# A new order of the instructions in the first fifteen slots of a fused attention and two-layer kernel

## The chip, the cores and the metric

The kernel runs on one core of a Trainium2 chip. The metric is the device time of one execution in microseconds. A core has five engines with queues of their own that work strictly in order: TensorE (PE in the profile; its weight loads are PEld), VectorE (DVE), ScalarE (ACT), GpSimd (POOL) and SyncE (SP), which here only issues DMAs. They meet through semaphores. TensorE writes to PSUM, eight banks of 128 x 512 floats, and another engine has to carry each result out before its bank can be written again.

## The reference

```python
def sm_attn(qq, kk, vv):                      # softmax attention, scale 1/8
    s = scale * qq @ kk.transpose(0, 1, 3, 2)
    a = np.exp(s - s.max(-1, keepdims=True))
    return (a / (a.sum(-1, keepdims=True) + 1e-9)) @ vv
pp  = sm_attn(p, k, v)                        # 8 batches x 8 heads, 32 packed rows x 64
out = sm_attn(q, pp, pp)                      # 576 rows per batch and head
x   = out.transpose(0, 2, 1, 3).reshape(4608, 512)
h = x @ w1_in;  y = (h * np.cos(h)) @ w1_out  # 512 -> 2048 -> 512
h = y @ w2_in;  g = P(h) / (Q(h) + 1e-6)      # P cubic; Q = 1 + |b0||h| + |b1|h^2
result = g @ w2_out                           # 4608 x 512
```

The four weight matrices arrive as 64-bit floats.

## The kernel before

**Stages.** First the packed attention (pp) of all batches, together with the second attention of batch 0 and the first conversions of weights, up to about 105 us. Then 128 *slots* for the first layer, eight batches of 576 rows, 16 slots a batch: a slot is one half of a batch's rows (288) and two blocks of 128 of the 2048 hidden columns. Last the second layer over 9 tiles of 512 rows. This case is about slots 0 to 14, between about 105 and 255 us of the span.

**Products in three passes.** Where the reference has one product of floats, the kernel has three with operands split into a rounded high part and the rest, hi x hi, hi x lo, lo x hi (`PASSES`). A split (`split`, `words_out`) is a copy on ScalarE (gh, hi of w1o, ah, yh) and a subtraction on VectorE or GpSimd (gl, lo of w1o, al, yl).

**W'.** The second attention's value product and the first layer's input product are merged: W' = pp x w1_in, per batch and head. It is made in 40 *units* (`wunit0` for batch 0, `wunit` for four or three other batches at a time). A unit of `wunit` is two matmuls into two PSUM banks of tag w, of which there are two in all. One half is scaled and copied out by ScalarE (line 316), the other by VectorE (line 314), into tiles `wev` (four), and a DMA writes them to the scratch `wd` (line 317). `fill(m)` issues m units.

**A slot** (`slot`, `chain1`, `mm_h`, `mm_y`). TensorE computes h (12 matmuls, line 614) into one tile of two banks, then y of the slot two back (24 matmuls in two halves, line 678) into the four banks y0 to y3, with units of W' between. The chain of the slot turns h into g = h cos h: ScalarE u (639), VectorE r (640), ScalarE absolute value and sine (645, 646), VectorE g (647). The split of g into gh and gl (66, 67, `finish_g`) is made in the chain of the *next* slot. From slot 11 (`LATE`) there are no units and h has two tiles.

**Conversions.** `conv_in` turns one block of 64-bit words (`words_in`) into floats: ScalarE (77), VectorE twice (79, 84), GpSimd (88). For w1_out the split by `words_out` (ScalarE 92, GpSimd 93) is put into a list, and `conv_out` issues one of it. The blocks come in the order of `steps`: f0 to f15 of w1_out, x8 to x15 of w1_in. y of slot n needs f blocks 2j and 2j+1. Slots 0 to 10 convert two blocks each (`conv_by`).

**Attention of batch 1** (`attn2_beside`) runs as a generator beside these slots: per head group a transpose of q (749, 753), scores on TensorE (763) with transposes back (771), maximum (777) and subtraction (778); then the exponential (783), sums (787 to 789), division (794), transposes (797) and splits (802, 812). `EARLY1` and `LATE1` say in which slots it is resumed.

**Order.** On TensorE, VectorE and ScalarE the instructions of this stretch stand in the order in which the code is written (`manual_schedule`); on GpSimd and SyncE a scheduler orders them.

Of the kernel before, what the change touches and what calls it, by code (L numbers as in the profile page):

```python
# [20 lines left out]
def pack_attention_moe_moe_kernel(  # L21
# [14 lines left out]
    nc = tc.nc  # L36
# [76 lines left out]
    if True:  # L113
# [152 lines left out]
        def ppt(n):  # L266
# [3 lines left out]
            for u in range(2):  # L270
# [7 lines left out]
                    out=to, in_=ps[r].rearrange("p (x u m) -> p u x m", u=2, m=M)[:, u], func=AF.Copy  # L278
                )

        def wunit0(fq, g):
            ps = psw.tile([128, 512], F32, tag="w", bufs=2, name="w")
# [15 lines left out]

        def wunit(Q, fq, hp):
            R = 128 if Q else 96  # L300
            both = [psw.tile([128, 512], F32, tag="w", bufs=2, name="w") for x in range(2)]
            for x, ps in enumerate(both):
                pace[0] = nc.tensor.matmul(  # L303
                    out=ps[0:R],
                    lhsT=wl[64 * x:64 * x + 64, Q, hp, 0:R],
                    rhs=w1i_t[fq][64 * x:64 * x + 64, hp],
                    start=True,
                    stop=True,
                    tile_position=(64 * x, 0),
                )  # L310
            for x, ps in enumerate(both):
                t = we_p.tile([128, 512], F32, tag="wev", bufs=WEV, name="wev")
                if x:
                    nc.vector.tensor_scalar(out=t[0:R], in0=ps[0:R], scalar1=INV2PI, scalar2=None, op0=ALU.mult)  # L314
                else:
                    nc.scalar.activation(out=t[0:R], in_=ps[0:R], func=AF.Copy, scale=INV2PI)
                nc.sync.dma_start(out=wd[fq][Q, hp, x, 0:R], in_=t[0:R])

        WEV = 4
        a_t, ppb_t = {}, {}  # L320

        def attn2_steps(b, pool, new_ps, tg, now, big=None):
# [336 lines left out]
        def mm_y(n, by_block=False):  # L659
# [11 lines left out]
            for u, d in steps:  # L671
                f = 2 * j + u
                if u == 1 and d == 0 and not by_block:
                    fill(1)
                    conv_out()
                    conv_by(n + 2)
                for i, (a, c) in enumerate(PASSES):
                    nc.tensor.matmul(  # L678
                        out=y_t[d][:, 0:HS],
                        lhsT=w1o_s[f // 4][a][:, f % 4, 128 * d:128 * d + 128],  # L680
                        rhs=gs[c][:, u],
                        start=(first and u == 0 and i == 0),
                        stop=(last and u == 1 and i == 2),
                    )
# [51 lines left out]
        def attn2_beside():  # L736
# [10 lines left out]
            for g in range(G):  # L747
# [10 lines left out]
                for hf in range(2):  # L758
# [16 lines left out]
                    yield  # L775
                mx = wk.tile([128, C], F32, tag="mx2", bufs=1, name="mx2")
                nc.vector.tensor_reduce(out=mx, in_=sT[g], op=ALU.max, axis=AX.X)
                nc.vector.tensor_tensor(
                    out=sT[g], in0=sT[g], in1=mx.unsqueeze(2).to_broadcast([128, C, M]), op=ALU.subtract
                )  # L780
                yield
            for g in range(G):
                nc.scalar.activation(out=sT[g], in_=sT[g], func=AF.Exp, scale=scale)
            yield
            sm = wk.tile([128, G, C], F32, tag="sm2", bufs=1, name="sm2")
            for g in range(G):
                nc.vector.tensor_reduce(out=sm[:, g], in_=sT[g], op=ALU.add, axis=AX.X)
            nc.vector.tensor_scalar(out=sm, in0=sm, scalar1=1e-9, scalar2=None, op0=ALU.add)
            nc.vector.reciprocal(out=sm, in_=sm)
            yield  # L790
            aT = wk.tile([128, G, C, 32], F32, tag="qT", bufs=1, name="aT")

            def turn(g):
                nc.vector.tensor_tensor(
                    out=sT[g], in0=sT[g], in1=sm[:, g].unsqueeze(2).to_broadcast([128, C, M]), op=ALU.mult
                )
                nc.vector.transpose(out=aT[:, g], in_=sT[g])

            ah = [a_p[b].tile([128, S], F32R, tag="ah", bufs=2, name="ah") for g in range(G)]

            def high(g):
                nc.scalar.activation(out=ah[g], in_=aT[:, g].rearrange("p c j -> p (c j)"), func=AF.Copy)

            turn(0)
            yield
            high(0)
            turn(1)
            yield
            high(1)
            for g in range(G):  # L810
# [4 lines left out]
                a_t[b, g] = (ah[g], al)  # L815
            yield

        EARLY1 = {2: 1, 4: 1, 5: 1, 7: 1}
        LATE1 = {1: 1, 2: 1, 3: 1, 5: 1, 6: 1, 8: 1, 9: 1, 10: 1, 11: 1}
        at1 = attn2_beside()  # L820

        def slot(n):
            nonlocal at
# [5 lines left out]
            if n >= LATE and y_ends(n - 2):  # L829
# [5 lines left out]
                else:  # L835
                    evict_y(n - 2, (0, 1))
                    next(parts)
                    evict_y(n - 2, (2, 3))
            else:
                next(parts)  # L840
                fill(1)
                next(parts)
                if n >= 2:
                    mm_y(n - 2)
                    if y_ends(n - 2):
                        evict_y(n - 2, range(NKD))
                else:
                    conv_out()
                    fill(2)
                    conv_by(n)  # L850
                for _ in range(EARLY1.get(n, 0)):
                    next(at1)
                fill(1)
                conv_by(n)
                conv_out()
                for _ in range(LATE1.get(n, 0)):
                    next(at1)
            if w2_out:
                w2_out.pop()()
# [38 lines left out]
        units += of(1) + of(2) + [(-1, fq, g) for fq in (2, 3) for g in range(G)] + of(3)  # L898
        at_u = [0]

        def fill(m):
            for _ in range(m):
                if at_u[0] < len(units):
                    Q, fq, hp = units[at_u[0]]
                    at_u[0] += 1
                    if Q < 0:
                        wunit0(fq, hp)
                    else:
                        wunit(Q, fq, hp)

        def conv_by(n):
            if n + 1 < len(steps):
                conv_in()


        for jj in range(NQ):
            wq_t[0, jj] = wo_p.tile([128, G, 2, 512], F32R, tag="wq", bufs=5, name="wq")
        by_hand.enter_context(
            tc.manual_schedule(engines={mybir.EngineType.Activation, mybir.EngineType.DVE, mybir.EngineType.PE})
        )  # L920
        next(at1)
        fill(5)
        for n in range(len(slots)):
            if n == LATE:
                assert at_u[0] == len(units)
                h_n[0] += 1
# [174 lines left out]
```

## Time and profile before

| | us |
|---|---|
| median of 3 runs (lowest, highest) | 1635.05 (1634.34, 1635.65) |
| profiled execution | 1637.78 |
| its span | 1636.0 |
| TensorE busy in the span | 1586.7 |
| VectorE, ScalarE busy | 1263.5, 1174.6 |
| slot 0 begins, slot 3 begins, slot 11 begins (first matmul of h) | 115.17, 151.68, 235.36 |

The span is what the profile covers; the profiled execution's time also has what lies around it. Times in the views count from the span's start. Matmuls are pipelined, so a busy TensorE need not be at full speed. "Busy" of the others is the time inside instructions; an engine that waits for a semaphore is idle.

### The profile page before, as it was taken

The numbers are of one execution on the slowest core, as the hardware profiler recorded it, in microseconds if no ns is written. First come the engines' busy times: TensorE is split into PE (matmuls) and PEld (weight loads), VectorE is DVE, ScalarE is ACT, GpSimd is POOL, SyncE is SP. The second block draws the span as 40 slices with busy tenths as digits, with TensorE's granted clock in tenths as the row PEclk, the third lists the DMA queues.
The fourth block names the chain that finished last, engine by engine and source line by source line (L and its number), as shares of the span: only waits on it lengthen the run. The fifth ranks groups of instructions, "written<-read, shape, count | busy, mean of one in ns | idle before, by whom it ended". The sixth has DMA issues, their size and how long they took to land.

```text
span 1636.0 us, 26266 instructions
## 1 busy us (share of the span) xinstructions
PE 1586.7 (97%) x9840; PEld 1342.4 (82%) x9840; DVE 1263.5 (77%) x1955; ACT 1174.6 (72%) x1958; POOL 161.5 (10%) x121
## 2 busy tenths in 40 slices
PE   6889999999999999999999999999999999999997
PEld 2445669999999999999988888888888888888886
DVE  5856788787878787878768888888888878888886
ACT  2465667676767677777667877777787777788775
POOL 0024241111111111202200000000000000000000
PEclk9898999999999999999999999999999999999999
DMA  9957875343434343335880201010101010020000
GB/s 265 261 187 231 256 216 163 106 137 109 134 115 128 119 124 121 122 120 171 293 306 1 72 7 55 24 52 26 52 26 52 26 47 31 1 74 5 17 10 26
DMA packets 99008, 175.40 MB, mean 107 GB/s; under 512 B 12736, under 2 KB 43968, under 8 KB 98880
## 3 DMA queue, kind: packets, MB, share of 16 engines
q1 hardware_dynamic: 98560, 173.19, 33.6%
q8 instruction: 78, 1.28, 0.3%
q10 hardware_dynamic: 320, 0.52, 0.1%
q14 instruction: 50, 0.41, 0.1%
HBM read 113.31 MB, written 60.36 MB: 106 GB/s over the span
## 4 chain that ended last, share of the span: by engine, by line
PE 84%; DVE 4%; issue 3%; ACT 2%; POOL 0%; DMA 0%; DVEq 0%; POOLq 0%
PE h L958 24%; PE o L1047 24%; PE y L678 21%; PE h L614 10%; PE w L303 2%; PE s L191 1%; DVE cvf L79 1%; DVE r L640 1%; DVE cvf L84 0%; ACT r L645 0%; ACT r L646 0%; DVE gl L67 0%; PE w L284 0%; PE s L763 0%; POOL cvf L88 0%
## 5 line engine op out<-in xcount | busy, mean ns | idle before, releaser
L678 PE MATMUL y<-gh,w1o 128*128 128x288 f32 x2048 | 433.1, 297 | 0.9 <-DVE yl L67 0.9
L958 PE MATMUL h<-x,w 128*128 128x512 f32 x1728 | 413.1, 393 | 0.0
L958 PEld LDWEIGHTS h<-x,w 128*128 128x128 f32 x1728 | 324.1, 188 | 74.6
L678 PEld LDWEIGHTS y<-gh,w1o 128*128 128x128 f32 x2048 | 336.8, 189 | 16.2 <-issue 14.8
L678 PE MATMUL y<-gl,w1o 128*128 128x288 f32 x1024 | 303.5, 296 | 2.4 <-DVE gl L67 2.3
L1047 PE MATMUL o<-w,g2h 128*128 128x512 f32 x1152 | 297.4, 393 | 1.3 <-ACT g2h L976 1.3
L1047 PEld LDWEIGHTS o<-w,g2h 128*128 128x128 f32 x1152 | 216.1, 188 | 51.3 <-ACT g2h L976 2.1
L614 PE MATMUL h<-ah,wq 128*128 128x288 f32 x1024 | 229.1, 299 | 0.9 <-DVE wev L314 0.9
L993 ACT ACTIVATE sq<-h 128x512 f32<-128x512 f32 x144 | 87.7, 609 | 175.6 <-PE h L958 175.4
L678 PEld LDWEIGHTS y<-gl,w1o 128*128 128x128 f32 x1024 | 194.0, 189 | 4.7 <-DVE gl L67 4.7
L614 PEld LDWEIGHTS h<-ah,wq 128*128 128x128 f32 x1024 | 172.1, 189 | 11.5 <-issue 5.2
L647 DVE SCALAR_TENSOR_TENSOR g<-h,r 128x576 f32<-128x576 f32 x128 | 96.9, 757 | 100.9 <-ACT r L646 100.9
L1047 PE MATMUL o<-w,g2l 128*128 128x512 f32 x576 | 164.2, 393 | 0.0
L639 ACT ACTIVATE u<-h,coef 128x576 f32<-128x576 f32 x128 | 94.0, 735 | 81.4 <-PE h L614 81.0
L614 PE MATMUL h<-al,wq 128*128 128x288 f32 x512 | 151.3, 296 | 0.0
L645 ACT ACTIVATE r<-r 128x576 f32<-128x576 f32 x128 | 87.8, 686 | 83.2 <-DVE r L640 83.2
L1004 DVE SCALAR_TENSOR_TENSOR ab<-ab,y 128x512 f32<-128x512 f32 x144 | 99.3, 689 | 55.8 <-ACT y L1001 55.7
L982 DVE TENSOR_TENSOR g2l<-c,g2h 128x512 fp32r<-128x512 f32 x144 | 99.1, 688 | 48.5 <-ACT g2h L976 46.5
L1047 PEld LDWEIGHTS o<-w,g2l 128*128 128x128 f32 x576 | 108.2, 188 | 24.4
L640 DVE SCALAR_TENSOR_TENSOR r<-u,h 128x576 f32<-128x576 f32 x128 | 95.1, 743 | 40.1 <-ACT u L639 39.1
L995 DVE SCALAR_TENSOR_TENSOR ab<-sq,coef,ab 128x512 f32<-128x512 f32 x144 | 107.5, 746 | 13.8 <-ACT ab L994 13.8
L996 ACT ACTIVATE c<-h,coef 128x512 f32<-128x512 f32 x144 | 113.8, 790 | 4.4 <-DVE g2l L982 4.4
(113 smaller groups left out, 2302.1 us busy)
## 6 DMA issues: line engine op xcount, KB each, us to landing
x<-yd SPq DMA_DIRECT2D x36, 512.0 KB
st<-in_moe_w_in_dram SPq DMA_DIRECT2D x32, 512.0 KB
st<-in_moe_w_out_dram SPq DMA_DIRECT2D x32, 512.0 KB
w<-w2d SPq DMA_DIRECT2D x64, 256.0 KB
wq<-wd SPq DMA_DIRECT2D x112, 128.0 KB
kx<-in_k_dram SPq DMA_DIRECT2D x16, 576.0 KB
vx<-in_v_dram SPq DMA_DIRECT2D x64, 144.0 KB
qx<-in_q_dram SPq DMA_DIRECT2D x16, 576.0 KB
```

The lines of the kernel that those rows point to most:

```text
L614: last_h[0] = nc.tensor.matmul(out=ps[:, u, 0:HS], lhsT=wq[:, g, a, o:o + 128], rhs=a_t[b, g][c][:, hf * HS:hf * HS + HS], start=(i == 0), ...
L639: nc.scalar.activation(out=u, in_=ph, func=AF.Identity, bias=coef[:, 6:7])
L640: nc.vector.scalar_tensor_tensor(out=r, in0=u, scalar=RND, in1=ph, op0=ALU.subtract, op1=ALU.subtract)
L645: nc.scalar.activation(out=r, in_=r, func=AF.Abs)
L647: nc.vector.scalar_tensor_tensor(out=gt, in0=ph, scalar=2.0 * math.pi, in1=r, op0=ALU.mult, op1=ALU.mult)
L678: nc.tensor.matmul(out=y_t[d][:, 0:HS], lhsT=w1o_s[f // 4][a][:, f % 4, 128 * d:128 * d + 128], rhs=gs[c][:, u], start=(first and u == 0 a ...
L958: nc.tensor.matmul(out=ps, lhsT=w2_s[f][:, 0, a, 128 * kk:128 * kk + 128], rhs=x_t[t, c, kk], start=(i == 0), stop=(i == 3 * NKD - 1),)
L982: nc.vector.tensor_tensor(out=gl, in0=gt, in1=gh.bitcast(F32), op=ALU.subtract)
L995: nc.vector.scalar_tensor_tensor(out=ab, in0=sq, scalar=coef[:, 5:6], in1=ab, op0=ALU.mult, op1=ALU.add)
L996: nc.scalar.activation(out=c1, in_=ph, func=AF.Identity, scale=coef[:, 3:4], bias=coef[:, 2:3])
L1004: nc.vector.scalar_tensor_tensor(out=ab, in0=ab, scalar=QC, in1=y0, op0=ALU.add, op1=ALU.mult)
L1047: nc.tensor.matmul(out=o_t[s], lhsT=g2_t[n][a][:, 128 * s:128 * s + 128], rhs=w2_s[f][:, 1, c], start=(f == 0 and i == 0), stop=(f == NFC ...
```

## The change

- `between(n)`, new, stands in the middle of y (or, in slots 0 and 1, between units): a unit, then the split of *this* slot's g (`finish_g(n)`), then up to two splits of w1o, then a conversion. Before, the split of g stood in the next slot ahead of a unit's eviction.
- `wunit` takes `vec`: which half VectorE evicts. In the middle of slots 2, 3, 4, 6 and 8 ScalarE evicts both, in slots 9 and 10 VectorE (slot 7's units are batch-0 units, which don't use it).
- `bank()`: the units up to slot 1 go round six banks, two of tag w and y0 to y3. Tiles `wev` are six instead of four.
- `sin_in()` applies the sine to one column, before the first units and right behind the exponential, so that ScalarE loads the sine's table there.
- `attn2_beside` has 17 steps instead of 14, resumed by `FIRST1`, `MID1` and `LAST1` up to slot 14.
- `CONV1`: the conversions of slot 7 go to slot 11; six units instead of five stand before slot 0, five instead of four in slots 0 and 1, two in slots 2, 5 and 7.

```diff
+        n_bank, on_y = [0], [True]
+
+        def bank():
+            i = n_bank[0] % 6 if on_y[0] else 0
+            n_bank[0] += 1
+            if i < 2:
+                return psw.tile([128, 512], F32, tag="w", bufs=2, name="w")
+            return ps1.tile([128, 512], F32, tag=f"y{i - 2}", name="w")
...
-        def wunit(Q, fq, hp):
+        def wunit(Q, fq, hp, vec):
...
-                if x:
+                if vec[x]:
                     nc.vector.tensor_scalar(out=t[0:R], in0=ps[0:R], scalar1=INV2PI, scalar2=None, op0=ALU.mult)
...
-        WEV = 4
+        WEV = 6
...
                 if u == 1 and d == 0 and not by_block:
-                    fill(1)
-                    conv_out()
-                    conv_by(n + 2)
+                    between(n + 2)
...
             for g in range(G):
                 nc.scalar.activation(out=sT[g], in_=sT[g], func=AF.Exp, scale=scale)
+            sin_in()
             yield
...
-        EARLY1 = {2: 1, 4: 1, 5: 1, 7: 1}
-        LATE1 = {1: 1, 2: 1, 3: 1, 5: 1, 6: 1, 8: 1, 9: 1, 10: 1, 11: 1}
+        def sin_in():
+            nc.scalar.activation(out=one, in_=coef[:, 7:8], func=AF.Sin, scale=0.0)
+
+        one = wk.tile([128, 1], F32, tag="one", bufs=1, name="one")
+        FIRST1, MID1 = (2, 5), (7,)
+        LAST1 = (1, 2, 3, 4, 5, 6, 7, 8, 9, 10, 11, 12, 14)
+        CONV1 = {n: 2 for n in range(12) if n != 7}
         at1 = attn2_beside()
+
+        def between(n):
+            if n < LATE:
+                fill(1, (n in (7, 9, 10), n in (0, 1, 5, 7, 9, 10)))
+                finish_g(n)
+            conv_out()
+            if n < LATE:
+                conv_out()
+            conv_by(n)
...
-            else:
+            elif n < LATE:
                 next(parts)
-                fill(1)
+                if n in FIRST1:
+                    next(at1)
+                else:
+                    fill(1, (n == 7, True))
                 next(parts)
+                if n in MID1:
+                    next(at1)
                 if n >= 2:
                     mm_y(n - 2)
+                    if n != 7:
+                        fill(1)
+                    conv_by(n)
                     if y_ends(n - 2):
                         evict_y(n - 2, range(NKD))
                 else:
-                    conv_out()
+                    fill(1)
+                    between(n)
+                    conv_by(n)
                     fill(2)
-                    conv_by(n)
-                for _ in range(EARLY1.get(n, 0)):
+                if n in LAST1:
                     next(at1)
-                fill(1)
+            else:
+                next(parts)
+                next(parts)
+                mm_y(n - 2)
...
         def conv_by(n):
-            if n + 1 < len(steps):
+            if n in CONV1:
                 conv_in()
...
+        sin_in()
         next(at1)
-        fill(5)
+        fill(6)
         for n in range(len(slots)):
+            on_y[0] = n < 2
```

How the order moves, at three places on VectorE. Line numbers of the changed kernel are 9 to 16 higher: 649, 656 and 323 there are 640, 647 and 314 here, and 786, 803, 807 and 811 are 778, 794, 797 and 812.

VectorE in slot 0, before: `wev` is an eviction of a unit, `r` and `g` the chain, `cvf` a conversion.

```order
L314 TENSOR_SCALAR wev<-w 96x512
L640 SCALAR_TENSOR_TENSOR r<-u,h 128x576
L314 TENSOR_SCALAR wev<-w 128x512
L647 SCALAR_TENSOR_TENSOR g<-h,r 128x576
L314 TENSOR_SCALAR wev<-w 96x512
L314 TENSOR_SCALAR wev<-w 128x512
L79 TENSOR_SCALAR cvf<-st_1504 128x512
L84 SCALAR_TENSOR_TENSOR cvf<-st_1504,cvf 128x512
L314 TENSOR_SCALAR wev<-w 96x512
L79 TENSOR_SCALAR cvf<-st_1517 128x512
L84 SCALAR_TENSOR_TENSOR cvf<-st_1517,cvf 128x512
L640 SCALAR_TENSOR_TENSOR r<-u,h 128x576
```

The same place in the changed kernel:

```order
L323 TENSOR_SCALAR wev<-w 96x512
L323 TENSOR_SCALAR wev<-w 128x512
L649 SCALAR_TENSOR_TENSOR r<-u,h 128x576
L323 TENSOR_SCALAR wev<-w 96x512
L656 SCALAR_TENSOR_TENSOR g<-h,r 128x576
L323 TENSOR_SCALAR wev<-w 128x512
L323 TENSOR_SCALAR wev<-w 96x512
L67 TENSOR_TENSOR gl<-g,gh 128x576
L79 TENSOR_SCALAR cvf<-st_1504 128x512
L84 SCALAR_TENSOR_TENSOR cvf<-st_1504,cvf 128x512
L79 TENSOR_SCALAR cvf<-st_1517 128x512
L84 SCALAR_TENSOR_TENSOR cvf<-st_1517,cvf 128x512
```

One eviction more stands ahead of the chain, the split gl now stands in the slot itself, and the first conversion behind it.

VectorE in slot 3, before, up to the attention's maximum `mx` and subtraction:

```order
L640 SCALAR_TENSOR_TENSOR r<-u,h 128x576
L67 TENSOR_TENSOR gl<-g,gh 128x576
L314 TENSOR_SCALAR wev<-w 96x512
L647 SCALAR_TENSOR_TENSOR g<-h,r 128x576
L314 TENSOR_SCALAR wev<-w 128x512
L79 TENSOR_SCALAR cvf<-st_1818 128x512
L84 SCALAR_TENSOR_TENSOR cvf<-st_1818,cvf 128x512
L314 TENSOR_SCALAR wev<-w 96x512
L79 TENSOR_SCALAR cvf<-st_1857 128x512
L84 SCALAR_TENSOR_TENSOR cvf<-st_1857,cvf 128x512
L777 TENSOR_REDUCE mx_1966<-sT 128x18
L778 TENSOR_TENSOR sT<-sT,mx_1966 128x576
```

Slot 3 in the changed kernel:

```order
L649 SCALAR_TENSOR_TENSOR r<-u,h 128x576
L323 TENSOR_SCALAR wev<-w 96x512
L656 SCALAR_TENSOR_TENSOR g<-h,r 128x576
L67 TENSOR_TENSOR gl<-g,gh 128x576
L79 TENSOR_SCALAR cvf<-st_1864 128x512
L84 SCALAR_TENSOR_TENSOR cvf<-st_1864,cvf 128x512
L323 TENSOR_SCALAR wev<-w 96x512
L79 TENSOR_SCALAR cvf<-st_1893 128x512
L84 SCALAR_TENSOR_TENSOR cvf<-st_1893,cvf 128x512
L786 TENSOR_TENSOR sT<-sT,mx_1895 128x576
```

gl moves from ahead of the first eviction to behind g, the second eviction is gone (ScalarE has it), and of the attention's two steps only the subtraction is left; the maximum stands at the end of slot 2.

VectorE in slot 11 up to r of slot 12, before:

```order
L640 SCALAR_TENSOR_TENSOR r<-u,h 128x576
L67 TENSOR_TENSOR gl<-g,gh 128x576
L647 SCALAR_TENSOR_TENSOR g<-h,r 128x576
L812 TENSOR_TENSOR al<-aT,ah 128x576 x2
L67 TENSOR_TENSOR wq<-wq 128x2x512
L640 SCALAR_TENSOR_TENSOR r<-u,h 128x576
```

Slot 11 in the changed kernel:

```order
L649 SCALAR_TENSOR_TENSOR r<-u,h 128x576
L656 SCALAR_TENSOR_TENSOR g<-h,r 128x576
L79 TENSOR_SCALAR cvf<-st_2633 128x512
L84 SCALAR_TENSOR_TENSOR cvf<-st_2633,cvf 128x512
L79 TENSOR_SCALAR cvf<-st_2662 128x512
L84 SCALAR_TENSOR_TENSOR cvf<-st_2662,cvf 128x512
L811 TENSOR_TENSOR al<-aT,ah 128x576
L803 TENSOR_TENSOR sT<-sT,sm_2364 128x576
L67 TENSOR_TENSOR wq<-wq 128x2x512
L649 SCALAR_TENSOR_TENSOR r<-u,h 128x576
```

Two conversions (f14 and f15), one of the two al and the second product of the division now stand between g of slot 11 and r of slot 12; gl of slot 10 is gone from here, and the other al stands in slot 14.

## Rows read from the trace of the kernel before

**Rows 1.** The page, busy us, share of the span and instructions by engine.
```profile
PE 1586.7 (97%) x9840; PEld 1342.4 (82%) x9840; DVE 1263.5 (77%) x1955; ACT 1174.6 (72%) x1958; POOL 161.5 (10%) x121
```

**Rows 2.** Windows cut at the slots: busy us (instructions) by engine, clock, DMA share, GB/s.
```profile
115.17:127.62 12.45, 10.19 (x29) 4.17 (x28) 5.11 (x8) 6.51 (x10) 0.80 (x1) 0.75 0.57 184
127.62:138.74 11.12, 9.58 (x30) 4.96 (x29) 6.81 (x11) 6.67 (x12) 4.28 (x4) 0.82 0.67 189
138.74:151.68 12.94, 12.52 (x81) 7.03 (x81) 10.30 (x16) 7.93 (x14) 6.59 (x6) 1.00 0.81 261
151.68:160.28 8.60, 8.60 (x52) 5.79 (x48) 5.57 (x9) 4.31 (x7) 3.91 (x3) 1.00 0.68 213
160.28:170.97 10.69, 9.49 (x51) 5.96 (x49) 9.30 (x13) 5.86 (x10) 3.90 (x4) 1.00 0.76 231
...
191.18:199.57 8.39, 8.39 (x50) 5.47 (x48) 7.85 (x12) 6.67 (x10) 1.73 (x2) 1.00 0.88 269
...
209.81:224.26 14.45, 12.53 (x50) 7.60 (x48) 9.99 (x15) 6.48 (x11) 6.58 (x5) 0.76 0.67 198
224.26:235.36 11.10, 9.68 (x51) 5.99 (x49) 9.33 (x14) 7.49 (x13) 5.69 (x4) 1.00 0.53 166
235.36:240.21 4.85, 4.85 (x37) 4.85 (x37) 4.33 (x6) 4.07 (x8) 3.65 (x4) 1.00 0.69 239
```

**Rows 3.** Chain that ended last, 213 to 236 us: start, length, what.
```profile
219.55 3.18 PE y L678 x12
...
225.02 0.42 DVE cvf L79
...
228.28 1.58 DVE gl L67
...
231.62 1.77 PE y L678 x12
233.39 1.11 PE w L303 x4
```

**Rows 4.** TensorE's waits from 106 to 236 us: total, times, longest.
```profile
PE w L303 <- ACT wev L316: 5.0, 6, 1.6
PE w L303 <- DVE wev L314: 2.8, 3, 1.9
```

**Rows 5.** Chain that ended last, 126 to 152 us.
```profile
141.18 1.29 DVE qT L749
...
147.74 1.10 PE s L763 x16
```

**Rows 6.** Timeline of ScalarE from 118.6 to 121.5 us: start, length, line, tiles.
```profile
118.62 0.68 ACT L645 ACTIVATE r<-r 128x576 f32<-128x576 f32 x1
119.32 1.28 ACT L646 ACT_TABLE_LOAD   x1
```

**Rows 7.** Instructions by form, 106 to 236 us: count, busy, mean ns, idle before.
```profile
L84 DVE SCALAR_TENSOR_TENSOR cvf<-st,cvf 128x512 uint32<-128x512 uint32 x22 | 15.3, 693 | 0.8
...
L79 DVE TENSOR_SCALAR cvf<-st 128x512 uint32<-128x512 uint32 x22 | 12.0, 545 | 0.0
L314 DVE TENSOR_SCALAR wev<-w 128x512 f32<-128x512 f32 x16 | 11.0, 685 | 8.9 <-PE w L303 7.8 <-PE y L678 1.0
...
L67 DVE TENSOR_TENSOR gl<-g,gh 128x576 fp32r<-128x576 f32 x10 | 9.4, 942 | 0.0
...
L647 DVE SCALAR_TENSOR_TENSOR g<-h,r 128x576 f32<-128x576 f32 x11 | 8.3, 756 | 6.2 <-ACT r L646 6.2
...
L778 DVE TENSOR_TENSOR sT<-sT,mx 128x576 f32<-128x576 f32 x2 | 2.8, 1397 | 0.1
```

**Rows 8.** Timeline of GpSimd and VectorE, 207.5 to 209.6 us.
```profile
207.94 1.28 POOL L93 TENSOR_TENSOR w1o<-cvf,w1o 128x512 fp32r<-128x512 f32 x1 [1.53 <-ACT w1o L92]
...
208.16 1.33 DVE L79 TENSOR_SCALAR cvf<-st 128x512 uint32<-128x512 uint32 x1
```

**Rows 9.** Instructions by line, 236 to 258 us.
```profile
L67 DVE TENSOR_TENSOR wq<-wq 128x1024 fp32r<-128x1024 f32 x2 | 2.4, 1218 | 0.1
```

More of the change, by code (lines that the diff above doesn't have):

```diff
@@ L279, in ppt @@
                 )
+        n_bank, on_y = [0], [True]
[5 more added lines that the diff above has]
+            return ps1.tile([128, 512], F32, tag=f"y{i - 2}", name="w")
         def wunit0(fq, g):
-            ps = psw.tile([128, 512], F32, tag="w", bufs=2, name="w")
+            ps = bank()
             for c in range(2):
@@ L297, in wunit0 @@
             )
-        def wunit(Q, fq, hp):
+        def wunit(Q, fq, hp, vec):
             R = 128 if Q else 96
-            both = [psw.tile([128, 512], F32, tag="w", bufs=2, name="w") for x in range(2)]
+            both = [bank() for x in range(2)]
             for x, ps in enumerate(both):
@@ L774, in attn2_beside @@
                     )
-                    yield
+                yield
                 mx = wk.tile([128, C], F32, tag="mx2", bufs=1, name="mx2")
                 nc.vector.tensor_reduce(out=mx, in_=sT[g], op=ALU.max, axis=AX.X)
+                yield
                 nc.vector.tensor_tensor(
@@ L787, in attn2_beside @@
                 nc.vector.tensor_reduce(out=sm[:, g], in_=sT[g], op=ALU.add, axis=AX.X)
+                yield
             nc.vector.tensor_scalar(out=sm, in0=sm, scalar1=1e-9, scalar2=None, op0=ALU.add)
             nc.vector.reciprocal(out=sm, in_=sm)
-            yield
             aT = wk.tile([128, G, C, 32], F32, tag="qT", bufs=1, name="aT")
-            def turn(g):
+            ah = [a_p[b].tile([128, S], F32R, tag="ah", bufs=2, name="ah") for g in range(G)]
+            for g in range(G):
                 nc.vector.tensor_tensor(
@@ L796, in turn @@
                 )
+                yield
                 nc.vector.transpose(out=aT[:, g], in_=sT[g])
-            ah = [a_p[b].tile([128, S], F32R, tag="ah", bufs=2, name="ah") for g in range(G)]
-            def high(g):
+                yield
                 nc.scalar.activation(out=ah[g], in_=aT[:, g].rearrange("p c j -> p (c j)"), func=AF.Copy)
[L804 to L810, printed above, removed]
                 al = a_p[b].tile([128, S], F32R, tag="al", bufs=2, name="al")
@@ L847, in slot @@
                 else:
-                    conv_out()
+                    fill(1)
+                    between(n)
+                    conv_by(n)
                     fill(2)
-                    conv_by(n)
-                for _ in range(EARLY1.get(n, 0)):
+                if n in LAST1:
                     next(at1)
-                fill(1)
+            else:
+                next(parts)
+                next(parts)
+                mm_y(n - 2)
+                if y_ends(n - 2):
+                    evict_y(n - 2, range(NKD))
                 conv_by(n)
                 conv_out()
-                for _ in range(LATE1.get(n, 0)):
+                if n in LAST1:
                     next(at1)
@@ L899, in pack_attention_moe_moe_kernel, with fill @@
         at_u = [0]
-        def fill(m):
+        def fill(m, vec=(False, True)):
             for _ in range(m):
@@ L908, in fill @@
                     else:
-                        wunit(Q, fq, hp)
+                        wunit(Q, fq, hp, vec)
         def conv_by(n):
-            if n + 1 < len(steps):
+            if n in CONV1:
                 conv_in()
```

## The prediction

> **What bounds it now.** I read the busy shares first, then the windows cut at the slots, then what TensorE waited for there, then the chain. Over the span TensorE is 97% busy [rows 1], so only the stretch where it is not can give anything back. In the windows that is the first eleven slots: slot 3 has TensorE busy for all of its 8.60 us, slot 11 for all of its 4.85 us, but slots 0, 1, 4, 9 and 10 have it busy for 9.5 to 12.5 us of 10.7 to 14.5 [rows 2]. A busy TensorE is not one at full speed: in slots 0, 1 and 9 the granted clock is 0.75 to 0.82, a mix of the 2.4 and 1.2 GHz levels, after gaps in its work, and 12 matmuls of y then take 3.18 us instead of 1.77 [rows 3].
>
> What ends those gaps is an eviction: W' units wait for the two PSUM banks of tag w, 5.0 us on ScalarE's copy and 2.8 us on VectorE's [rows 4]. The chain shows what stands ahead of the eviction on VectorE's queue. At 228.28 it is the split gl, 1.58 us [rows 3]; at 141.18 the query transpose [rows 5]. VectorE is fuller than any other helper here: 9.30 of 10.69 us in slot 4 (87%), 9.33 of 11.10 in slot 10 (84%) [rows 2]. So the stretch is a queueing problem between TensorE and VectorE.
>
> **The work of TensorE does not change.** It is the same 40 units, 11 h and 9 y. A unit is 1.11 us, a half y 1.77 [rows 3], one half of the scores 1.10 [rows 5]. So a floor for the new slots 3 to 10 follows: 8.60 for a slot with three units, 8.39 where they are the batch-0 units (old slot 7), one unit less in slots 5 and 7 and two half scores in slot 5: 8.6 + 8.6 + 9.7 + 8.6 + 7.3 + 8.4 + 8.6 + 8.6 = 68.4 us, for 22 units. The old slots 3 to 10 took 235.36 - 151.68 = 83.7 us for 24 units [rows 2].
>
> **Opening, slots 0 and 1, and scores of slot 2.** With six banks TensorE can run three units ahead, so it stops waiting bank by bank, and the sine table (1.28 us, until now between absolute value and sine of slot 0 [rows 6]) is loaded while the first matmuls run. What is late next is VectorE: up to the query transpose it has 12 evictions x 0.685, four r and g x 0.756, two gl x 0.942, four conversions x (0.545 + 0.693) [rows 7] and 1.29 for the transpose [rows 5], 19.4 us, and two waits for a sine that I put at 0.75 each, 20.9 us. Its first W' eviction should come about 114, a little before the old slot 0 starts at 115.17 [rows 2], so the scores can start at about 135. Behind the eviction that frees the last unit's banks VectorE still has three evictions, gl, two conversions and the transpose, 6.8 us, and TensorE only that unit and h(2), 1.11 + 1.77: it stands for about 4 us in front of the scores. The rest of slot 2 is 2 x 1.10 + 2 x 1.77 + 2 x 1.11 = 8.0 us, and up to 2.8 more if the two half y run at the lower clock; I take 1.8. So slot 3 begins at 145 (143 to 147) instead of 151.68, with 18 units done instead of 16.
>
> The W' writes grow denser. 24 tiles are 5.4 MB and two loads of weights 1.0 MB; slot 2 moved 261 GB/s at a DMA share of 0.81 [rows 2], so 6.4 MB need 20 to 24.5 us. That lies beside VectorE's 21 and costs nothing at the lower end, 4 us at the upper, where six eviction buffers run out.
>
> **Slots 3 to 10.** By the new order VectorE's work per slot, with 0.42 for an undisturbed L79 [rows 3], can be added up: slot 3 has r, g and gl at 0.75, two evictions, two conversions and the subtraction, 1.40 [rows 7], 7.3 us. Slots 3 to 10 come to 7.3, 7.4, 7.5, 7.3, 4.4, 6.6, 8.3 and 8.0 us. At the 85% that it reached in its fullest slots this is 8.6, 8.7, 8.9, 8.6, 5.2, 7.8, 9.8, 9.4. The larger of this and the floor, slot by slot, sums to 70.5. Slot 7 gets both table loads (2 x 1.28) and both exponentials on ScalarE with only 7.3 us of TensorE above them: 1 us more.
>
> Then the port. An L79 that meets a running GpSimd instruction takes 1.33 us, from 208.16 until just after GpSimd ends at 209.22 [rows 8]; the 22 of today average 0.545 [rows 7]. In the new order two splits of w1o are issued directly ahead of the first conversion of a slot, so GpSimd tends to be running when L79 comes. I charge 0.9 in slots 3, 4, 9 and 10, where VectorE is the bound, less what waits anyway: 2.5 us. Sum 74 us, between 68.4 and 82. Slot 11 then begins at 145 + 74 = 219 instead of 235.36: 16 us earlier.
> The Trainium skill, "SBUF — State Buffer", section "SBUF: two separate sides", says that VectorE and GpSimd share one port pair as an exclusive lock and that the loser blocks for the whole instruction, also where a VectorE instruction has two SBUF inputs. The trace agrees for L79 (1.33 us) and for gl (1.58 us). That speaks against putting two GpSimd splits ahead of gl's successors, and is a rival below.
>
> **Slots 11 to 13: a wait that is new.** The conversions of slot 7 move to slot 11, those of f14 and f15. There TensorE has only 4.85 us of work. VectorE now has r, g, two conversions, one al, one product, and the split of wq (1.22 us [rows 9]): 0.76 + 0.76 + 2 x 1.11 + 2 x 0.75 + 1.22 = 6.5 us, and about 1.4 of waiting for absolute value and sine (0.68 for the first [rows 6]), so r of slot 12 starts about 8 us after r of slot 11, not 4.85. ScalarE's rounded halves of f14 and f15 stand behind the sine of slot 12 (two entries that I put at 0.65, like the 0.68 above), then GpSimd has two splits of 1.28 [rows 8]: about 13 us after r of slot 11. TensorE wants f15's low half for y(11) after h(12), y(10) and h(13), about 9 us after it. I charge 4.5 us, 0 to 7. The attention steps that move into slots 12 and 14, a transpose and a split, are under 1 us each beside the 4.85 us that TensorE has in a slot there, and I count them as hidden; if slot 11's queue is still full behind them, that is in the upper end of 7.
>
> **Sum.** 16.4 earlier at slot 11, 4.5 given back, 0.9 rounded off for gaps at the lower clock: 11 us. After slot 16 nothing changes. The profiled execution took 1637.78 us (span 1636.0), 2.7 over the median of the runs, 1635.05; the difference goes on the median: 1624 us.
>
> **Rivals.**
> - The order hides nearly all waits: slot 3 at 143, then the floor, and f15 in time: 143 + 68.4 = 211.4, 24 us: 1611. For it: old slots 3 and 7 do run at the floor. Against: the fullest VectorE slots do not.
> - The port rules: each of the eight slots pays 1 us more than 71.5 in its conversions and gl. 145 + 79.5 + 4.5 = 229 against 235.36: 6 us, 1629. For it: 1.33 and 1.58 above. Against: today's 22 L79 lose (0.545 - 0.42) x 22 = 2.8 us in all.
> - DMA is the bound in slots 0 and 1: scores at 139, 4 us lost: 1628. Against: the DMA share was 0.57 and 0.67 there [rows 2].
> - Slower: VectorE stands at gl. Until now gl of a slot was done in the next slot, when gh was long ready. Now it stands in the same slot, behind a gh that ScalarE makes only after the two evictions of the middle unit, and both conversions, an eviction and the attention step queue behind gl. If VectorE's round is then r to gl 5.6 (r, eviction, g, gl, and waits for sine, unit and gh) plus 5.4 for the rest, 11 us, eight slots take 88: 145 + 88 + 4.5 = 237.5, 2 to 3 us over 235.36: 1638. From 10.7 us a slot the gain is gone. Against: a VectorE that is late finds gh ready, so the wait shrinks as it falls behind.
> - Nothing happens: evictions were only named last, and the stretch is limited by ScalarE's and VectorE's sum: 1635.
>
> **Chances.** Forecast 0.48, floor 0.15, port 0.12, DMA 0.08, gl 0.10, nothing 0.07. The forecast's own range is 1618 to 1630. Leaving out the slow case and the outer part of the floor gives 1613 to 1634. What a measurement can tell from no change is about 0.2%, 3.3 us. Faster by more: 0.82; within: 0.08; slower: 0.10.
>
> **What would show it.** Right: no table load between absolute value and sine in slot 0; scores of slot 2 near 135 behind the query transpose; slot 3 near 145; slots 3 to 10 at 8.6 to 10 us; TensorE waiting at y of slot 13 for w1o's low half from GpSimd. Wrong: slot 3 later than 150, slots over 10.5 us with VectorE idle ahead of gl, or L79 mostly above 1 us.

## The result, and the profile after

The changed kernel is slower. Its median is 1649.07 us (four runs, 1646.44 to 1652.41) against 1634.69 for the kernel before (four runs, 1631.02 to 1635.65): a ratio of 1.0093 over all runs, 95% interval 1.0068 to 1.0118. The forecast was 1624, with 1634 as the upper end of its range. The profiled execution took 1647.92 us, its span 1646.1.

Cut at the slots (a slot begins with its first h matmul), the stretch shows the place. These are the windows of the changed kernel, with the columns of [rows 2] (length, busy us and instructions of TensorE, its weight loads, VectorE, ScalarE and GpSimd, then clock, DMA share, GB/s):

```profile
110.11:117.52 7.41, 7.39 (x35) 3.51 (x33) 4.63 (x8) 5.80 (x10) 0.00 (x0) 1.00 0.87 277
117.52:126.67 9.15, 8.67 (x33) 3.74 (x32) 7.02 (x11) 5.64 (x11) 2.63 (x2) 1.00 0.89 280
126.67:145.72 19.05, 11.62 (x78) 7.07 (x77) 12.33 (x16) 8.24 (x16) 6.41 (x5) 0.82 0.61 206
145.72:156.80 11.08, 10.49 (x50) 6.17 (x48) 9.26 (x11) 6.99 (x12) 5.70 (x5) 1.00 0.59 167
...
191.40:198.70 7.30, 7.30 (x47) 5.35 (x45) 5.21 (x8) 5.50 (x8) 3.02 (x2) 1.00 0.93 283
...
217.70:233.71 16.01, 10.87 (x50) 6.36 (x49) 14.88 (x18) 7.44 (x13) 8.49 (x7) 0.96 0.64 191
233.71:241.03 7.32, 7.32 (x37) 7.32 (x38) 4.06 (x6) 3.21 (x6) 2.87 (x5) 0.62 0.84 301
241.03:247.60 6.57, 5.02 (x38) 4.79 (x37) 6.50 (x6) 3.87 (x7) 5.42 (x4) 1.00 0.38 124
247.60:259.70 12.10, 8.08 (x38) 7.27 (x37) 8.56 (x12) 6.16 (x11) 2.79 (x3) 0.72 0.29 94
```

Slots 0 and 1 are as short as hoped: 7.41 and 9.15 us against 12.45 and 11.12 [rows 2]. Slot 2 gives most of that back (19.05 for 12.94), slot 10 takes 16.01 us with VectorE busy for 14.88 of them, and slots 11 to 13, which took under 5 us each before, take 26.0 together. The same sums from the profiles of the kernels that matter below, in us from the first h matmul of slot 0:

| | before | changed | changed, GpSimd's work out (a4) | before, GpSimd's work out (b4) | best reordering (a9) |
|---|---|---|---|---|---|
| slots 0, 1 | 23.57 | 16.56 | 17.39 | 25.69 | 16.55 |
| slot 2 | 12.94 | 19.04 | 15.02 | 12.27 | 18.39 |
| slots 3 to 10 | 83.68 | 87.99 | 72.73 | 75.65 | 82.25 |
| slots 11 to 13 | 14.37 | 25.99 | 16.50 | 14.38 | 14.90 |
| slots 0 to 13 | 134.56 | 149.59 | 121.64 | 128.00 | 132.10 |

The 15.0 us between the first two columns are close to the difference of the medians, 14.4. The two profiled executions differ by only 10.1 in their spans, because slot 0 began 5.1 us earlier in the changed kernel's, at 110.11 instead of 115.17; behind slot 13 both take the same time, 1386.4 and 1386.3 us. Where slot 0 begins scatters from profile to profile (see the opening, below), so the slots are counted from its start.

What grew is seen in VectorE's groups of instructions by line (count, sum in us, mean in ns; 106 to 262 us of the changed kernel):

```profile
L79 DVE TENSOR_SCALAR cvf<-st 128x512 uint32<-128x512 uint32 x22 | 23.0, 1047 | 0.0
L84 DVE SCALAR_TENSOR_TENSOR cvf<-st,cvf 128x512 uint32<-128x512 uint32 x22 | 22.0, 999 | 0.8
L649 DVE SCALAR_TENSOR_TENSOR r<-u,h 128x576 f32<-128x576 f32 x14 | 10.4, 741 | 3.7 <-ACT u L648 3.7
L323 DVE TENSOR_SCALAR wev<-w 128x512 f32<-128x512 f32 x15 | 10.1, 682 | 1.2 <-DMA wd<-wev 1.2
```

The same 22 L79 and 22 L84 had means of 545 and 693 ns [rows 7]: 27.3 us have become 45.0. The evictions and r, which read PSUM, are as long as ever. VectorE's timeline at the beginning of slot 3 and GpSimd's beside it show how:

```profile
144.65 0.76 DVE L67 TENSOR_TENSOR gl<-g,gh 128x576 fp32r<-128x576 f32 x1 [3.45 <-ACT gh L66]
145.33 1.51 DVE L79 TENSOR_SCALAR cvf<-st 128x512 uint32<-128x512 uint32 x1
146.88 1.65 DVE L84 SCALAR_TENSOR_TENSOR cvf<-st,cvf 128x512 uint32<-128x512 uint32 x1
148.45 0.68 DVE L323 TENSOR_SCALAR wev<-w 128x512 f32<-128x512 f32 x1
```

```profile
145.22 2.77 POOL L93 TENSOR_TENSOR w1o<-cvf,w1o 128x512 fp32r<-128x512 f32 x2 [10.51 <-ACT w1o L92]
148.66 1.28 POOL L88 TENSOR_TENSOR cvf<-cvf,st 128x512 uint32<-128x512 uint32 x1 [0.68 <-DVE cvf L84]
```

The pair of subtractions (two of 1.4 us) starts just ahead of the conversion. L79 lets the first pass and L84 the second: 3.2 us for what takes 0.42 + 0.69 undisturbed. I call the excess of VectorE's instructions over an undisturbed one of their kind, summed from 104 to 265 us, its *blocked time*: 9.8 us before, 25.7 after. What is taken as undisturbed moves such a sum by up to 1.6 us. (The expectations below quote 8.6 and 24.5; there the subtraction of the maximum still counted as undisturbed at 1.34 us, which after showed to be 0.75.)

What follows from it in slot 10 is told by VectorE's timeline there, and by TensorE's waits from 106 to 262 us (sum, times, longest):

```profile
217.20 1.52 DVE L79 TENSOR_SCALAR cvf<-st 128x512 uint32<-128x512 uint32 x1
218.75 1.65 DVE L84 SCALAR_TENSOR_TENSOR cvf<-st,cvf 128x512 uint32<-128x512 uint32 x1
220.33 0.68 DVE L323 TENSOR_SCALAR wev<-w 96x512 f32<-96x512 f32 x1
220.93 1.24 DVE L79 TENSOR_SCALAR cvf<-st 128x512 uint32<-128x512 uint32 x1
222.21 0.69 DVE L84 SCALAR_TENSOR_TENSOR cvf<-st,cvf 128x512 uint32<-128x512 uint32 x1
...
223.44 1.59 DVE L803 TENSOR_TENSOR sT<-sT,sm 128x576 f32<-128x576 f32 x1
224.96 0.74 DVE L649 SCALAR_TENSOR_TENSOR r<-u,h 128x576 f32<-128x576 f32 x1
...
229.79 1.49 DVE L79 TENSOR_SCALAR cvf<-st 128x512 uint32<-128x512 uint32 x1
231.32 1.64 DVE L84 SCALAR_TENSOR_TENSOR cvf<-st,cvf 128x512 uint32<-128x512 uint32 x1
232.88 0.68 DVE L323 TENSOR_SCALAR wev<-w 128x512 f32<-128x512 f32 x1
```

```profile
PE s L770 <- DVE ppT L760: 11.0, 2, 7.4
PE h L623 <- DVE wev L323: 3.3, 1, 3.3
PE y L685 <- ACT w1o L92: 3.1, 1, 3.1
PE w L312 <- DVE wev L323: 2.6, 4, 1.4
PE y L685 <- POOL w1o L93: 2.4, 2, 1.5
```

r could have started about 220.4, when ScalarE's u was done, and stands behind the queue until 224.96; the eviction that frees the bank for the next h stands behind a second blocked conversion until 232.88, and TensorE waits 3.3 us. Before, the largest of TensorE's waits here were for evictions, 5.0 and 2.8 us [rows 4]. The longest wait of all is new: 7.4 us in slot 2, ahead of the scores, while four conversion instructions from 128.00 to 133.20 took 5.2 us instead of 2.2 and the transposes of q and pp queued behind them. Behind that wait the granted clock is 0.50, the lower of the two levels (1.2 GHz), from 135.9 to 140.1 us, and the two half scores take 4.06 us, not twice the 1.10 of [rows 5].

### The profile page after: what moved, and what is told of

It reads as the page before. It is cut to its first block, busy times and chain, and to the rows that moved or that the text cites. A ratio compares the mean times of both kernels' runs of the same rounds, so it can differ in the third digit from the quotient of the medians.

```text
span 1646.1 us, 26266 instructions
## 1 busy us (share of the span) xinstructions
PE 1583.0 (96%) x9840; PEld 1346.6 (82%) x9840; DVE 1275.2 (77%) x1952; ACT 1177.0 (71%) x1963; POOL 162.6 (10%) x121
## 3 DMA queue, kind: packets, MB, share of 16 engines
q8 instruction: 78, 1.28, 0.3%
## 4 chain that ended last, share of the span: by engine, by line
PE 78%; issue 2%; DVE 2%; ACT 1%; DMA 0%; POOL 0%; DVEq 0%; POOLq 0%
PE h L987 24%; PE o L1076 24%; PE y L685 20%; PE h L623 9%; PE s L191 1%; DVE cvf L79 1%; DVE r L649 0%; ACT r L655 0%; ACT r L654 0%; DVE wq L67 0%; DMA st<-in_moe_w_out_dram 0%; DVE gl L67 0%; DVE yl L67 0%; DVE cvf L84 0%; POOL cvf L88 0%
```

## The experiments

Each result is a median, then the ratio of the runs to those of the kernel before on the same chip, with the 95% interval. The kernel before had medians of 1632.93 to 1636.89 us in these comparisons, so two kernels of different comparisons are better compared by their ratios.

**First: which part of the order?** The theory at that point was that conversions stand behind the pair of subtractions; the rivals were the missing conversions of slot 7 and the place of the scores.

```diff
# a1: in between()                      # a2
+            conv_by(n)                 -CONV1 = {n: 2 for n in range(12) if n != 7}
             conv_out(); conv_out()     +CONV1 = {n: 2 for n in range(11)}
-            conv_by(n)
# a3: slots 2 and 5: a unit where the scores were, the scores at the slot's end
# b1: the kernel before, with bank(), six wev, sin_in(), five units in slots 0 and 1;
#     slots 2 and later in the old order, three units fewer in slots 2, 5 and 9
```

> The changed kernel, but in the middle of a slot the conversion stands ahead of the two splits of w1o. Port theory (VectorE's conversion steps L79 and L84 are blocked by GpSimd's L93 pair; their sum rose from 27 to 45 us): L79 + L84 fall to 30 to 36 us, the time falls by 5 to 10 us against the changed kernel, to about 1641. Rival (the f14/f15 conversions in slot 11 are what costs): no more than 2 us, since slots 11 to 13 keep their 26 us.

Measured 1648.41 us, 1.0076 (1.0054 to 1.0099). L79 fell to 16.5 us, L84 rose to 24.9: the sum of 41.4 lies above the 30 to 36 expected. The block moved from one instruction to the next; with four GpSimd instructions of 1.3 us in a slot, the adds of the first conversion meet the second. The gain of 5 to 10 us did not come either.

> The changed kernel with the conversions of slot 11 back in slot 7. Late-conversion theory: slots 11 to 13 go from 26.0 us back towards 14.4, TensorE's waits for w1o there (3.1 us on ScalarE's, 2.4 us on GpSimd's) vanish, and the time falls by 7 to 11 us, to 1638 to 1642. Port theory alone: slots 7 to 10 pay it back, since the conversions only move into a stretch where VectorE is already blocked: within 3 us of 1649.

Measured 1645.67 us, 1.0069 (1.0042 to 1.0096). Slots 11 to 13 came back to 15.9 us, and slot 8 went from 10.24 to 15.85. The wait was moved, not removed, and the time lies between the two ranges.

> The changed kernel with a unit ahead of y in slots 2 and 5 and the scores at the slot's end, behind y. Early-scores theory: TensorE's two waits for the ppT transpose (11.0 us) and the lower clock behind them go, slots 2 and 5 fall from 19.0 and 15.8 to 12 to 14 us, the time by 5 to 9 us, to 1640 to 1644. Port theory: VectorE is late for other reasons and TensorE waits for evictions in place of ppT; less than 3 us.

Measured 1644.15 us, 1.0054 (1.0033 to 1.0075). Slot 5 fell from 15.84 to 11.52, slot 2 only from 19.04 to 18.20, and slot 8 rose to 13.75. Of the two slots only slot 5 did what was expected.

> The kernel before with the opening alone: six banks up to slot 1, six eviction buffers, the early sine table, six units first and five in slots 0 and 1, the two conversions of slots 0 and 1 ahead of their splits; slots 2 and up in the old order, three units fewer in slots 2, 5 and 9. If the opening is a gain that the rest throws away (slot 2 began 12 us earlier in the changed kernel): 6 to 12 us under the kernel before, 1623 to 1629. If VectorE's sum binds the whole stretch: within 3 us of 1635.

Measured 1633.42 us, 0.9978 (0.9962 to 0.9993): the opening alone is a small gain, not the 6 to 12 us expected; the time is in the rival's range. Its slots 0 and 1 take 16.56 us, slot 2 17.09: there too the pair runs in front of the transposes (L79 1.47 us, L84 1.66).

**Second: is it GpSimd at all?** The work itself was taken out, from the changed kernel and, as control, from the one before.

```diff
# a4, b4: conversions of w1_in and w1_out
-        nc.vector.scalar_tensor_tensor(out=f, in0=up, ...)
-        nc.gpsimd.tensor_tensor(out=out, in0=f, in1=dn, op=ALU.add)
+        nc.vector.scalar_tensor_tensor(out=out, in0=up, ...)
-        nc.gpsimd.tensor_tensor(out=lo, in0=v, in1=hi, op=ALU.subtract)
+        nc.gpsimd.memset(lo, 0.0)
# a5: one conv_out() in between(), one at the slot's end
# b2, on the kernel before: second conv_out() of a slot in the middle of y, ahead of conv_by
```

> The changed kernel with GpSimd's two operations of the weight conversions of W1 left out: the add of the low word (L88) and the low half of w1_out (L93), which is set to zero instead. Its result is therefore not the reference's. Theory P (the changed order puts VectorE's evictions and conversions beside GpSimd's instructions, and the shared port blocks them): nearly all of the loss goes, slots 2 to 10 fall from 107 us to 88-94 us, the time comes to 1615-1628 us and L79 and L84 keep to 0.55 and 0.70 us. Theory O (the order of the instructions itself is the loss: VectorE's queue is too full and too strictly in order, port or no port): the time stays at 1640-1648 us, the slots of 15 us and more stay, with a PE wait for VectorE in each.

Measured 1617.88 us, 0.9899 (0.9881 to 0.9918); slots 2 to 10 take 87.7 us.

> The kernel before with the same operations left out (L88's add and L93, low half set to zero; its result is not the reference's). It is the control for the other: what counts is the changed kernel against this one. Theory P: this one gains little, since its own blocked time is 8.6 us and half of it off the path: 1627-1634 us, and the changed one without these operations is 5 to 12 us faster than this one. Theory O: the changed one stays 8 to 15 us slower than this one.

Measured 1621.01 us, 0.9916 (0.9898 to 0.9935): 6 us below what I had put for it. The pair of results decides for theory P all the same. With GpSimd's work the new order costs 14.4 us; without it, it is 3.1 us ahead (1616.57 to 1618.75 against 1618.19 to 1622.54). That is less than the 5 to 12 expected, and the two sets of runs just overlap, so the times show that the loss goes, and not that the order by itself gains. Both leave the work out ahead of slot 0 as well, so the table's slots are the cleaner measure: 15.0 us behind with it, 6.4 ahead without. VectorE's blocked time is about 2 us in either, and slots 3, 4 and 6 of the changed kernel fall to 8.5 us. L79, 106 to 262 us, changed kernel without GpSimd's work:

```profile
L79 DVE TENSOR_SCALAR cvf<-st 128x512 uint32<-128x512 uint32 x24 | 10.7, 445 | 0.0
```

> The changed kernel with the two splits of a slot apart again, one in the middle of the slot and one at its end as in the kernel before, everything else as changed. Theory P with the pair of GpSimd subtractions as its cause: blocked VectorE time falls from 24.5 us to 12-15, the time to 1638-1643 us. Theory O: within 3 us of the changed kernel, 1645-1650 us.

Measured 1644.06 us, 1.0061 (1.0040 to 1.0081); blocked time 17.0 us. Between the two theories: slots 11 and 12 are back, slot 4 is 14.51 for 9.86.

> The kernel before with only the two splits of a slot put together in the middle of the slot (slots 2 to 10), ahead of the conversion there; nothing else changed. Theory P with the pair as its cause: blocked VectorE time rises from 8.6 us to 15-20, slots 2 to 10 get 4 to 10 us longer, 1639-1645 us. Theory O: 1633-1637 us, since nothing but the place of two ScalarE and two GpSimd instructions has moved.

Measured 1634.95 us, 1.0004 (0.9984 to 1.0024). The blocked time did rise, to 16.8 us, and the time did not. So the pair alone is not enough, and blocked time has no fixed price: in the old order 7 us more of it cost nothing that could be measured.

**Third: a block or a wait for results?** Taking the work out also takes away what ScalarE and TensorE wait for. One kernel keeps every GpSimd instruction, with results that nobody reads; three more move the subtractions to where VectorE reads PSUM.

```diff
# a6: VectorE's L84 writes the result; GpSimd's add goes to a spare place;
#     TensorE reads w1_out's high half for both halves
# a7: in slot(), between() without conv_out in slots 2 to 10
                 next(parts)
+                conv_out()
                 ...
                 next(parts)
+                conv_out()
# a8 = a7 and a3;  a9 = a8 and a2
```

> The changed kernel with GpSimd's instructions of the W1 conversions all in their places and of their sizes, but with results that nobody waits for: the add of the low word goes to a spare place, and the low half of w1_out is written but not read (the matmuls read the high half twice). Its result is therefore not the reference's. Theory B (GpSimd costs by blocking VectorE's instructions at the shared port): the loss of the changed kernel stays, 1638-1650 us, blocked VectorE time 18-26 us. Theory W (GpSimd costs because ScalarE and the y matmuls wait for its results): close to the run without GpSimd's work, 1617-1624 us.

Measured 1646.64 us, 1.0081 (1.0057 to 1.0106), blocked time 25.9 us: nearly the whole loss (1.0093 in the changed kernel), with nobody waiting for GpSimd. TensorE's waits and VectorE's L79 are nearly those of the changed kernel, and no wait of TensorE is for GpSimd:

```profile
PE s L778 <- DVE ppT L768: 11.2, 2, 7.6
PE y L693 <- ACT w1o L98: 4.9, 1, 4.9
PE h L631 <- DVE wev L329: 3.3, 1, 3.3
```

```profile
L79 DVE TENSOR_SCALAR cvf<-st 128x512 uint32<-128x512 uint32 x22 | 23.2, 1055 | 0.0
```

> The changed kernel with the two splits of a slot (slots 2 to 10) moved ahead by half a slot: one right behind the first step of the chain (ScalarE's u, VectorE's r), one right behind its second (g). GpSimd's subtractions then run beside VectorE instructions that read PSUM (r, g, the evictions), which were never lengthened beside GpSimd, and not beside gl, L79 and L84. Theory B: blocked VectorE time falls from 24.5 us to 8-14, the time to 1630-1640 us. Theory W: within 4 us of the changed kernel, 1645-1653 us.

Measured 1641.43 us, 1.0036 (1.0020 to 1.0052); blocked time 17.7 us; both lie above the ranges given, the time by 1.4 us and the blocked time by 3.7. Slot 10 falls from 16.01 to 11.98, slot 5 from 15.84 to 12.58.

> As the one before, and the scores of the attention in slots 2 and 5 at the slot's end instead of in front of the chain's second step. Theory B: what is left in the two slots is TensorE's wait for ppT behind VectorE's queue, so another 3-5 us less than the kernel with the splits early alone, 1626-1636 us. Theory W: 1641-1648 us, as the late scores alone gave 4 to 5 us.

Measured 1638.23 us, 1.0025 (1.0009 to 1.0041): 3.2 us less, 2 over the range. Slot 5 is 10.89, but slot 2 still 17.90.

> As the one before, and two conversions in slot 7 too (none left for slot 11). Theory B: slots 11 to 13 come back to 14.5-16 us, slot 7 or 8 pays 1 to 3 us of it, so 1624-1634 us. Theory W: 1638-1646 us.

Measured 1630.90 us, 0.9976 (0.9961 to 0.9991), blocked time 13.3 us. With three changes of order, and the same work, the changed kernel is now slightly ahead of the one before. Slots 11 to 13 take 14.9 us; the debt is in slot 8, 15.96 us.

**Last.** What was open: whether VectorE's time counts alike when it is blocked and when it works, and what keeps slot 8 long.

```diff
# a10, on a9: low halves of slots 2 to 10 on VectorE, behind gl
-        nc.gpsimd.tensor_tensor(out=lo, ...)
+        nc.vector.tensor_tensor(out=lo, ...)
# a11, on a9: no conversion in between() of slot 7, one left for slot 11
```

> The best reordering so far (splits early, late scores, conversions in slot 7 too) with the low halves of slots 2 to 10 on VectorE, behind gl, instead of on GpSimd. VectorE works 0.7-0.75 us for each and GpSimd keeps only the adds of the low word. Theory V (VectorE's occupied time counts, blocked or working): what the clash gives back, about 6 us, is spent again as 7 us of work, so 1628-1634 us, level with that kernel (1630.9). Theory C (only clashes hurt, VectorE has time to spare): 1621-1627 us.

Measured 1639.30 us, 1.0026 (1.0011 to 1.0041). Neither range holds it. Ten low halves at 0.68 us are 6.8 us more work, and the time is about 8 us over a9's (1.0026 against 0.9976), so VectorE has no time to spare and theory C falls. But the clash gave nothing back: blocked time is 14.0 us, since in a9's order the subtractions no longer met anything that they block. What still blocks are mostly the adds, L88: 11 of the 15 blocks in a9.

> The same best reordering with one conversion in slot 7 instead of two, the other in slot 11. If the second conversion there makes slot 8 long: slot 8 falls from 15.96 to 10.5-12.5 us, slots 11 to 13 rise by 0 to 2, so 1626-1630 us. If the exponential of slot 7 does it (VectorE idle for 3.8 us ahead of wq's eviction): slot 8 stays over 14 us and the time at 1630-1634.

Measured 1636.44 us, 1.0005 (0.9991 to 1.0019). Slot 8 stays at 15.43, and slot 13 rises to 11.05, 6 us where 0 to 2 were allowed, so the time is over both ranges. The second conversion of slot 7 is not what keeps slot 8 long. VectorE's timeline in slot 8 of a9 (slot 8 of a11 begins with the same wait of 3.80 us):

```profile
198.88 0.69 DVE L303 SCALAR_TENSOR_TENSOR wq<-w,wq 128x512 fp32r<-128x512 f32 x1 [3.80 <-ACT wq L302]
199.48 0.75 DVE L67 TENSOR_TENSOR gl<-g,gh 128x576 fp32r<-128x576 f32 x1
200.15 0.42 DVE L79 TENSOR_SCALAR cvf<-st 128x512 uint32<-128x512 uint32 x1
200.60 0.69 DVE L84 SCALAR_TENSOR_TENSOR cvf<-st,cvf 128x512 uint32<-128x512 uint32 x1
201.21 0.42 DVE L79 TENSOR_SCALAR cvf<-st 128x512 uint32<-128x512 uint32 x1
201.67 1.65 DVE L84 SCALAR_TENSOR_TENSOR cvf<-st,cvf 128x512 uint32<-128x512 uint32 x1
203.24 0.74 DVE L796 TENSOR_REDUCE sm<-sT 128x18 f32<-128x576 f32 x1
203.91 0.74 DVE L649 SCALAR_TENSOR_TENSOR r<-u,h 128x576 f32<-128x576 f32 x1
```

It begins with 3.80 us in which VectorE waits for a copy of ScalarE's that stands behind two table loads and the exponentials; all that is behind it, r of the slot last, comes late. With no conversion in slot 7 (a8) slot 8 takes 12.17 us, so both have a part.

## Why the prediction was wrong

**The step that failed is the port.** For slots 3 to 10 the sum was a fullness of VectorE, 70.5, plus 1 for slot 7, plus 2.5 for the port. Without GpSimd's work these slots take 72.7 us against 71.5: as a sum, what stands beside the port was sized well. (Slot by slot less so: five of the eight take 7.3 to 8.5 us, no more than TensorE's floor, while slot 5 takes 11.7 where 9.7 was put and slot 8 9.9 where 8.4 was.) With GpSimd's work they take 88.0, so the port's term is 15.3 us, not 2.5. I had charged 0.9 us to four slots, for L79 alone. The trace shows L84 blocked for as long (0.69 to 1.65), the second L79 of a slot beside L88, and the division by the sums (0.75 to 1.59 in slot 10). One of the prediction's own signs of being wrong is there: L79 takes more than 1 us in 14 of 22 cases.

For slots 0 to 13 the forecast's terms add up to 122.7 us, and they take 149.6. Of the 26.9 us between, 14.0 lie in slots 3 to 10, 7.1 in slots 11 to 13 and 5.8 in slots 0 to 2. Without GpSimd's work the same order takes 121.6, so nearly the whole miss goes with that work; the other two parts are told below.

The Trainium skill, "SBUF — State Buffer", section "SBUF: two separate sides", names VectorE instructions with two SBUF inputs beside those in a two-port mode as losers of the shared lock, against a GpSimd instruction that reads SBUF. That rule was cited in the prediction, and the trace agrees: L84 has two such inputs and took 1.65 us. It was applied to gl and not to L84, since L84's mean of 693 ns [rows 7] had no block in it. That was the order's doing: before, 5 of 22 L79 and no L84 were blocked, after, 15 and 7.

**The rival of the port rules** had the right mechanism and the wrong price and sign: 1 us a slot, 1629. It counted the delay of the blocked instruction and not that GpSimd had four instructions a slot, and VectorE nothing to spare. The rival with a VectorE round of 11 us came to 88 us for the eight slots, which is what they took, but by luck and not by its mechanism: it had VectorE idle ahead of gl, and gl waited 7.0 us in all, against 15.9 us more of blocked time.

**The opening.** The forecast had slot 3 begin at 145, and it began at 145.72, which looks like a hit and is not. It rested on the old slot 0 starting at 115.17 [rows 2]. That start scatters from profile to profile: 111.51 with the old order (b2), 108.0 to 114.4 with the new opening. From slot 0 on, slots 0 to 2 took 35.6 us, not 145 - 115.17 = 29.8. Without GpSimd's work they took 32.4, so about half of the 5.8 us is the port again (5.2 us for four conversion instructions ahead of the transposes). The wait in front of the scores was 7.4 us, where 4 was the forecast.

**Slots 11 to 13** gave back 11.6 us (26.0 - 14.4), where 4.5 was charged and 7 was the upper end. Without GpSimd's work it is 2.1 (16.50 - 14.37), and with two conversions in slot 7 0.5 (a9). The mechanism was the one described, y waiting for f14 and f15; the size was not, because al and the product there met the port as well. TensorE's waits for the two halves of w1o are 5.5 us (3.1 and 2.4 above). About as much is the lower clock, which the sum had only as 0.9 rounded off: slot 11 has no wait in it and takes 7.32 us instead of 4.85, at a mean granted clock of 0.62, behind the 3.3 us that TensorE waited at the end of slot 10. VectorE in slots 12 and 13:

```profile
243.30 1.69 DVE L84 SCALAR_TENSOR_TENSOR cvf<-st,cvf 128x512 uint32<-128x512 uint32 x1
244.91 1.81 DVE L811 TENSOR_TENSOR al<-aT,ah 128x576 fp32r<-128x576 f32 x1
246.65 1.86 DVE L803 TENSOR_TENSOR sT<-sT,sm 128x576 f32<-128x576 f32 x1
248.43 1.21 DVE L67 TENSOR_TENSOR wq<-wq 128x1024 fp32r<-128x1024 f32 x1
249.56 0.74 DVE L649 SCALAR_TENSOR_TENSOR r<-u,h 128x576 f32<-128x576 f32 x1
```

Undisturbed, the first three are 2.2 us, not 5.4; r of slot 12 and with it ScalarE's copies of f14 and f15 come that much later, and TensorE, having waited, then ran slot 13 at a mean granted clock of 0.72.

**What was right:** no wait bank by bank in slots 0 and 1, and the table load gone from there (the sine follows the absolute value at once, at 114.28). DMA was not the limit: its share was 0.87 and 0.89 there, and slots 0 and 1 were short all the same.

**What stays open** is the price of a blocked microsecond. It is 7 us for nothing in b2, and about one for one in slots 3 to 10 of the changed kernel taken together (15.3 us lost beside some 15 us of blocked time there), but not slot by slot: slot 5 loses 4.1 us against a4 with 0.8 blocked in it. Slot 10 takes 11.64 us with 2.5 blocked (a9), 16.33 with 3.6 (a5) and 16.01 with 5.4 (changed). That it is decided by which wait of TensorE ends last is my reading and not shown, and I have no rule that gives it beforehand.

## What to carry to other kernels

When an order puts one engine's instructions together, ask what runs beside them, instruction by instruction, and not only whether the mean of today is short: a mean without blocks says that the old order kept the two apart. Before trusting a gain in an order, take the suspected neighbour's work out of both kernels; the pair of runs tells the order's own worth from the collision. Count slots from a common event, not in absolute times of one profile.

## What the hardware showed

- An elementwise VectorE instruction with SBUF operands alone (L79, L84, gl, al, the attention's subtraction and product) lets a running add or subtraction of GpSimd end before it starts its work: L79 0.42 us alone and up to 1.56 beside GpSimd, L84 0.69 and up to 1.69, al 0.75 and 1.81. Those that read PSUM are not touched: 16 evictions beside GpSimd took 0.68 us like 13 alone, and r took 0.74 in both. Transposes and reductions of SBUF weren't touched either (1.37 us for q's transpose, 0.75 for the maximum). The rule has no exception in these sixteen kernels, 104 to 265 us: of the instructions that began with 0.2 us or more of a GpSimd add or subtraction still to run, all 135 L79 and all 76 L84 were longer than alone, and none of 97 evictions and 98 r was.
- What GpSimd does matters. In a4 and b4 it fills tiles with a constant (memset, 0.53 us, no tile is read). L79 was longer beside these too, 0.53 to 0.75 us in three cases. The five instructions with two SBUF inputs that began with 0.2 us or more of a memset still to run (L84 twice, gl, yl twice) took their usual time. The cases are few.
- GpSimd pays too: L93 took 1.26 to 1.28 us alone or beside instructions that read PSUM, 1.44 on average before and 1.46 after, and up to 1.89 where VectorE was at one of the instructions above as it began.
- In slot 3 a pair of GpSimd instructions back to back blocked two VectorE instructions, one each: VectorE gets in between the two, and is blocked again.
